# Experts sorted by load on the chip, with capacities of 448, 416, 416 and five times 384 tokens in place of 512 for each

## The chip, the cores and the metric

One core of one Trainium2 chip runs the kernel. The metric is the device time of one execution in microseconds (us); less is better. The profile gives the span from the first to the last instruction of one profiled execution; the device time of that execution lies a little above its span.

## The reference

A recurrent attention block is followed by a mixture of experts. `r`, `k` and `v` have 4 batches, 8 heads, 768 steps and a head size of 48; the attention's output, with heads joined, is a matrix `x` of N = 3072 tokens by 384. Each token goes to the one of 8 experts whose embedding has the largest cosine with it. The expert is a two-layer network (384 to 1024, relu, 1024 to 384), and its output is scaled by the token's softmax weight.

```python
for t in range(S):
    cur = einsum('bhd,bhe->bhde', u * k_t, v_t)
    y[:, :, t] = einsum('bhd,bhde->bhe', r_t, state + cur)
    state = w * state + einsum('bhd,bhe->bhde', k_t, v_t)
x = y.transpose(0, 2, 1, 3).reshape(3072, 384)
logits = normalized(x) @ normalized(expert_emb).T / tau
expert_idx = argmax(logits, axis=1)
gate_w = softmax(logits)[arange(N), expert_idx]
for e in range(8):
    mask = expert_idx == e
    h = maximum(x[mask] @ w1[e], 0)
    out[mask] = gate_w[mask, None] * (h @ w2[e])
```

All is float32. Counted on the reference's own inputs, the experts 0 to 7 get 352, 386, 373, 408, 427, 374, 380 and 372 tokens. After the first 4 of the 6 steps of 128 positions the counts are 247, 251, 253, 271, 272, 248, 256 and 250.

## The kernel before

The attention works in 24 units of 128 tokens (6 chunks of the sequence by 4 batches). The order of the work is written out by hand: `attention` (L544) is a loop over a step `i`, and each step runs one stage of several units. TensorE (PE) transposes r and k (`turn`, L259 and L264), makes scores (`scores`, L277), sums (`sums`, L324 and L327) and states (L294), ScalarE (ACT) copies and makes the diagonal rows (`own_rows`, L249), VectorE (DVE) masks (L281) and adds (`rows`, L340), GpSimd (POOL) scales k (L226) and makes `KU` (L234, L235). Four units of one chunk form a group. For each group `choose`, `ranks`, `gates` and `places` find the expert, the place in the expert's list and the gate of each of its 512 tokens; `cum` holds the running counts (L482). `listed` and `taken` turn places into lists: two one-hot tiles are multiplied on PE (L523, the lanes stationary, 64 columns), and `summed` adds the result to `sums`, a tile of 128 lanes by 2 by 32 slots (token number and gate). An expert has TM = 4 slots of 128 lanes, so 512 places.

PSUM tiles of the attention have one buffer for each tag (two for `tp` and `at`). The tag `st` is shared by the states, by `rank` and by `take`.

The finished rows are stored to DRAM (`put`, L488, on SyncE's DMA queue, SP). The same queue loads K, R and V five units ahead and, in steps 4 and 8, the weights of experts 0 and 1. Constants are made once at the start (`build_consts`), on DVE and POOL, before DVE's first step of unit 0 (L261).

The experts follow in their own order 0 to 7 (L805). For each, POOL gathers four tiles of 128 rows by indirect DMA (L608), PE transposes them (L624, 12 transposes), and DVE copies (L625). The first layer has the weights stationary and 512 tokens as columns: 24 products (L630), each of them two PE instructions in the profile. The second layer has the tokens stationary and 384 output columns: 32 products (L635), again two instructions each. DVE scales by the gate (L637), and POOL scatters 128 rows (L638). The weights have two buffers; those of expert e + 2 are loaded when expert e has released its own (L200, L201). Places with no token are skipped by the bounds check of the DMA.

At the end `needs` counts (L649 to L656) whether an expert has more than 512 tokens, and `again` reads a flag on every engine and jumps past a slow general path, which loops over all experts, unless the flag is set.

Of the kernel before, what the change touches and what calls it, by code (L numbers as in the profile page):

```python
# [18 lines left out]
N = B * S  # L19
# [6 lines left out]
TM = 4  # L26
TT = N // 128
SKIP = 1 << 20
SLOTS = E * TT
W_MIN, W_MAX = 0.7, 1.4  # L30
# [75 lines left out]
def build_consts(k):  # L106
# [33 lines left out]

    k.pos = pool.tile([128, NCH, B], I32, name="pos")
    k.gate = pool.tile([128, NCH, B], F32, name="gate")
    k.sums = pool.tile([128, 2, E * TM], F32, name="sums")
    nc.vector.memset(k.sums, 0.0)

# [51 lines left out]

def load_weights(k, e, tiles):
    w1, w2 = tiles
    k.nc.sync.dma_start(out=w1, in_=k.w1[e].rearrange("(c p) f -> p c f", p=128))  # L200
    k.nc.sync.dma_start(out=w2, in_=k.w2[e].rearrange("(f p) m -> p f m", p=128))  # L201
# [318 lines left out]
def taken(k, g):  # L520
    g.take = k.ps.tile([128, 2, E * TM], F32, name="take", tag="st")
    for b in range(B):
        k.nc.tensor.matmul(  # L523
            g.take.rearrange("p q s -> p (q s)"), g.lane[:, b, :], g.what[:, b].rearrange("p q s -> p (q s)"),
            start=(b == 0), stop=(b == B - 1),
        )


def summed(k, g):
    k.nc.vector.tensor_add(k.sums, k.sums, g.take)  # L530

# [11 lines left out]
def attention(k):  # L543


    units = B * NCH

    def on(f, i):
        if 0 <= i < units:
            f(k, i)  # L550

    def of_group(f, i):
        if 0 <= i < units:
            f(k, k.groups[i // B], i % B)

    def whole(f, i):
        if 0 <= i < units and i % B == B - 1:
            f(k, k.groups[i // B])

    emb = build_experts(k)  # L560
    for i in range(-1, units + 7):
        if 0 < i + AHEAD < units:
            load(k, i + AHEAD)
        if i in (B, 2 * B):
            load_weights(k, i // B - 1, k.weights[i // B - 1])
        if i < 2:
# [12 lines left out]
        on(carry, i)  # L579
        on(rows, i)  # L580
        of_group(put, i)
        on(scores, i + 1)
        on(own_sum, i + 1)
        of_group(turn_rows, i - 1)
        of_group(logits, i - 2)
        whole(ranks, i - 3)
        whole(gates, i - 3)
        whole(taken, i - 5)
        if i == B:
            decays(k)  # L590

# [11 lines left out]
def gather(k, take, gate):  # L603
# [5 lines left out]
        out=G[:, :], out_offset=None, in_=k.xs[:, :], in_offset=IndirectOffsetOnAxis(ap=take, axis=0),  # L609
        bounds_check=N - 1, oob_is_err=False,  # L610
    )
    return G, take, gate


def expert(k, rows, w1, w2):
# [3 lines left out]
    n = 128 * len(rows)  # L619
    xT = k.xtp.tile([128, NK, TM * 128], F32, name="xTe", tag="xTe")  # L620
    for m in range(NK):
        ps = k.ps.tile([128, TM * 128], F32, name="ps", tag="ps")
        for t, (G, _, _) in enumerate(rows):
            nc.tensor.transpose(ps[:, t * 128 : (t + 1) * 128], G[:, m * 128 : (m + 1) * 128], k.ident)  # L624
# [7 lines left out]
    for t, (_, take, gate) in enumerate(rows):  # L632
        ps = k.ps.tile([128, DM], F32, name="ps", tag="ps")
        for f in range(NF):
            mm(ps, hT[:, f, t * 128 : (t + 1) * 128], w2[:, f, :], start=(f == 0), stop=(f == NF - 1))  # L635
        y = k.gp.tile([128, DM], F32, name="y", tag="y", bufs=4)
        nc.vector.tensor_scalar_mul(y, ps, gate)  # L637
        nc.gpsimd.indirect_dma_start(  # L638
            out=k.out[:, :], out_offset=IndirectOffsetOnAxis(ap=take, axis=0), in_=y[:, :], in_offset=None,
            bounds_check=N - 1, oob_is_err=False,  # L640
        )


def needs(k, first):


    nc, pool = k.nc, k.const
    cp = k.ps.tile([128, E], F32, name="ps", tag="ps")
    nc.tensor.matmul(cp, k.ones, k.cum, start=True, stop=True)  # L649
    count = pool.tile([1, E], F32, name="count", tag="count", bufs=2)  # L650
    nc.vector.tensor_sub(count, cp[0:1, :], k.ebase)
    need = pool.tile([1, E, TG], F32, name="need", tag="need", bufs=2)
    for g in range(TG):
        nc.vector.tensor_scalar(need[:, :, g], count, float(TM * 128 * g), None, ALU.is_gt)
    if not first:
        nc.vector.memset(need[:, :, 0], 0.0)  # L656
    return need
# [24 lines left out]
def again(k, need):  # L682


    nc, tc = k.nc, k.tc
# [7 lines left out]
    with tc.If(left > 0):  # L693
        nc.sync.dma_start(out=k.need_dram.rearrange("e g -> (e g)").unsqueeze(0), in_=as_int(k, need))
        far = nc.values_load(flag[0:1, 1:2], min_val=0, max_val=1)
        with tc.If(far > 0):
# [6 lines left out]
            with ExitStack() as ctx:  # L703
                expert_pools(k, ctx)
                nc.sync.dma_start(out=k.need_dram.rearrange("e g -> (e g)").unsqueeze(0), in_=as_int(k, needs(k, True)))
        all_lists(k)
        with ExitStack() as ctx:
            expert_pools(k, ctx)
            with tc.For_i(0, E, 1) as e:
# [7 lines left out]
                nc.sync.dma_start(out=w1, in_=k.w1[bass.ds(e, 1)].rearrange("o (c p) f -> p (o c) f", p=128))  # L717
                nc.sync.dma_start(out=w2, in_=k.w2[bass.ds(e, 1)].rearrange("o (f p) m -> p (o f) m", p=128))
# [36 lines left out]
def kernel(  # L755
# [46 lines left out]
    with ExitStack() as ctx2:  # L802
        expert_pools(n, ctx2)
        take = tiles(n, n.sums, E * TM)
        for e in range(E):  # L805
            at = [gather(n, take[:, j : j + 1], n.sums[:, 1, j : j + 1]) for j in range(e * TM, (e + 1) * TM)]
            expert(n, at, *n.weights.pop(0))
            if e + 2 < E:
                n.weights.append(weight_tiles(n))
                load_weights(n, e + 2, n.weights[-1])  # L810
        need = needs(n, False)
    again(n, need)


# [26 lines left out]
```

## Time and profile before

| | us |
|---|---|
| median of 3 runs | 557.59 |
| lowest, highest | 557.38, 567.32 |
| the profiled execution, device time | 562.05 |
| its span | 560.3 |
| attention, first product to the last list (about) | 0 to 193 |
| first product of the first expert | 202.01 |
| end of the last expert's last product (about) | 545.9 |

The span is the number the parts below add up to. The device time of that execution is 1.75 us above it, and the median of the three runs is 4.46 us below that device time. A row of the chain or of the timeline has a start, a length, an engine and a line of the kernel; a count behind x says how many instructions were merged.

### The profile page before, as it was taken

The numbers are of one execution on the slowest core, as the hardware profiler recorded it, in microseconds if no ns is written. First come the engines' busy times: TensorE is split into PE (matmuls) and PEld (weight loads), VectorE is DVE, ScalarE is ACT, GpSimd is POOL, SyncE is SP. The second block draws the span as 40 slices with busy tenths as digits, with TensorE's granted clock in tenths as the row PEclk, the third lists the DMA queues.
The fourth block names the chain that finished last, engine by engine and source line by source line (L and its number), as shares of the span: only waits on it lengthen the run. The fifth ranks groups of instructions, "written<-read, shape, count | busy, mean of one in ns | idle before, by whom it ended". The sixth has DMA issues, their size and how long they took to land.

```text
span 560.3 us, 7017 instructions
## 1 busy us (share of the span) xinstructions
PE 532.2 (95%) x2625; PEld 355.6 (63%) x2625; DVE 163.1 (29%) x409; ACT 122.1 (22%) x361; POOL 175.5 (31%) x246
## 2 busy tenths in 40 slices
PE   8899999999999589999999999999999999999990
PEld 4899999999999444554554554554554564564550
DVE  6666666666565320030030030030020020010011
ACT  1465444444454002002002002002002102102100
POOL 5856656666651270121122022022022020010010
PEclk9999999999896559999999999999999999999995
DMA  9879796545100040341332322323313312000010
GB/s 188 158 155 305 149 300 133 115 106 115 47 32 30 3 119 1 126 138 44 128 119 69 128 98 82 128 73 112 128 55 131 128 33 106 6 36 1 1 41 8
DMA packets 94590, 54.26 MB, mean 97 GB/s; under 512 B 77741, under 2 KB 89198, under 8 KB 94546
## 3 DMA queue, kind: packets, MB, share of 16 engines
q1 hardware_dynamic: 89024, 43.85, 28.7%
q0 software_dynamic: 4096, 9.45, 5.2%
q10 hardware_dynamic: 1426, 0.41, 0.3%
q8 instruction: 23, 0.38, 0.3%
q14 instruction: 21, 0.17, 0.1%
HBM read 45.83 MB, written 11.01 MB: 101 GB/s over the span
## 4 chain that ended last, share of the span: by engine, by line
PE 91%; DVE 3%; issue 1%; ACT 1%; DMA 1%; POOL 0%; POOLq 0%; ACTq 0%
PE ps L630 30%; PE ps L635 29%; PE y L327 7%; PE at L277 5%; PE y L324 3%; PE st L294 3%; PE lg L433 2%; PE wake L60 2%; PE ps L624 2%; PE xp L418 2%; PE rt L259 2%; PE kt L264 1%; DVE AT L281 1%; PE take L523 1%; ACT xd L249 1%
## 5 line engine op out<-in xcount | busy, mean ns | idle before, releaser
L630 PE MATMUL ps<-xTe,w 128*128 128x512 f32 x384 | 169.6, 602 | 0.5 <-DVE xTe L625 0.5
L635 PE MATMUL ps<-w,hT 128*128 128x384 f32 x512 | 166.4, 486 | 0.0
L635 PEld LDWEIGHTS ps<-w,hT 128*128 128x128 f32 x512 | 97.3, 190 | 69.5 <-issue 3.8
L630 PEld LDWEIGHTS ps<-xTe,w 128*128 128x128 f32 x384 | 73.2, 192 | 92.3 <-issue 86.0
L638 POOL DMA_INDIRECT out_dram<-y,take x32 | 31.7, 991 | 272.9 <-DVE y L637 268.8
L637 DVE TENSOR_SCALAR y<-ps,sums 128x384 f32<-128x384 f32 x32 | 19.8, 618 | 302.5 <-PE ps L635 302.5
L631 ACT ACTIVATE hT<-ps 128x512 f32<-128x512 f32 x64 | 38.2, 597 | 300.7 <-PE ps L630 289.2
L249 ACT ACTIVATE xd<-V,diag 128x48 f32<-128x48 f32 x192 | 45.9, 321 | 20.0 <-DVE diag L241 15.4
L327 PE MATMUL y<-V,AT 128*128 128x48 f32 x384 | 47.5, 278 | 0.0
L327 PEld LDWEIGHTS y<-V,AT 128*128 128x128 f32 x384 | 46.5, 198 | 0.0
L608 POOL DMA_INDIRECT G<-xs,take x32 | 32.6, 1018 | 19.6 <-PE ps L630 8.6
L281 DVE TENSOR_TENSOR AT<-at,umask 128x512 f32<-128x512 f32 x48 | 30.9, 686 | 13.4 <-PE at L277 13.4
L311 POOL TENSOR_TENSOR state<-state,wpow 48x192 f32<-48x192 f32 x40 | 20.4, 509 | 31.1 <-DVE state L307 29.6
L277 PE MATMUL at<-RT,KT 48*128 48x128 f32 x384 | 27.9, 285 | 1.9 <-ACT KT L266 1.9
L277 PEld LDWEIGHTS at<-RT,KT 48*128 48x128 f32 x384 | 23.3, 187 | 3.6 <-ACT KT L266 2.6
L235 POOL TENSOR_TENSOR KU<-KU,Rpad 128x384 f32<-128x384 f32 x24 | 24.1, 1002 | 1.9
L234 POOL TENSOR_TENSOR KU<-K,u_bc 128x384 f32<-128x384 f32 x24 | 23.9, 998 | 0.3 <-DVE diag L241 0.3
L420 ACT COPY xT<-xp 128x384 f32<-128x384 f32 x24 | 11.5, 478 | 56.6 <-PE xp L418 56.6
L226 POOL TENSOR_TENSOR Kpad<-K,kpow 128x384 f32<-128x384 f32 x23 | 22.9, 997 | 1.2
L294 PE MATMUL st<-V,Kpad 128*128 128x96 f32 x160 | 21.7, 281 | 0.7 <-DVE at L478 0.7
L324 PE MATMUL y<-state,RT 128*128 128x96 f32 x160 | 22.0, 282 | 0.0
L294 PEld LDWEIGHTS st<-V,Kpad 128*128 128x128 f32 x160 | 20.3, 199 | 1.4 <-DVE at L478 1.4
(119 smaller groups left out, 393.0 us busy)
## 6 DMA issues: line engine op xcount, KB each, us to landing
w<-in_moe_w_dram SPq DMA_DIRECT2D x16, 1536.0 KB, 7.7
K<-in_k_dram SPq DMA_DIRECT2D x24, 192.0 KB, 3.9
V<-in_v_dram SPq DMA_DIRECT2D x24, 192.0 KB, 4.1
xs<-X SPq DMA_DIRECT2D x24, 192.0 KB, 2.0
Rpad<-in_r_dram SPq DMA_DIRECT2D x23, 192.0 KB, 4.2
G<-xs,take POOLq DMA_INDIRECT x32
out_dram<-y,take POOLq DMA_INDIRECT x32
Rpad<-in_r_dram ACTq DMA_DIRECT2D x1, 192.0 KB, 3.5
```

Of the source, the lines that this page charges most:

```text
L235: nc.gpsimd.tensor_mul(KU, KU, R[:, :, 0:D])
L249: k.nc.scalar.mul(xd[:, h, :], V[:, h, :], diag[:, h : h + 1])
L277: nc.tensor.matmul(at[s][:, p, :], KT[rows, p, :], RT[rows, p, :], start=True, stop=True)
L281: nc.vector.tensor_mul(a, at[s], k.umask[:, None, :].to_broadcast([128, NP, C]))
L294: nc.tensor.matmul(st[:, p, :], pair(Kw, p), pair(V, p), start=True, stop=True)
L324: mm(pair(y, p), RT[:, p, :], T[:, p, :], start=first, stop=False, skip_group_check=True)
L327: mm(y[:, h, :], AT[h % 2][:, h // 2, :], V[:, h, :], start=first, stop=(h == H - 1), skip_group_check=True,)
L608: nc.gpsimd.indirect_dma_start(out=G[:, :], out_offset=None, in_=k.xs[:, :], in_offset=IndirectOffsetOnAxis(ap=take, axis=0), bounds_check ...
L630: mm(ps[:, 0:n], w1[:, m, f * 128 : (f + 1) * 128], xT[:, m, 0:n], start=(m == 0), stop=(m == NK - 1))
L631: nc.scalar.activation(hT[:, f, 0:n], ps[:, 0:n], ACT.Relu)
L635: mm(ps, hT[:, f, t * 128 : (t + 1) * 128], w2[:, f, :], start=(f == 0), stop=(f == NF - 1))
L638: nc.gpsimd.indirect_dma_start(out=k.out[:, :], out_offset=IndirectOffsetOnAxis(ap=take, axis=0), in_=y[:, :], in_offset=None, bounds_chec ...
```

## The change

The lists are kept turned: `taken` has the one-hot of the slots stationary and the lanes as 128 columns, and `sums` is 64 by 128. After four of the six chunks (step 19) one small product counts the tokens of each expert (`counted`), and in step 20 `settle` ranks the counts on DVE. The two experts with the fewest tokens by then are fixed as ranks 7 and 6, their numbers go into a register of SyncE, and their weights are loaded then, in place of the loads in steps 4 and 8. At the end of the attention the counts are taken again, the other six are ranked by load, and a product with a permutation (`turned_lists`, `lists`) turns the lists back, in the order of ranks. The experts run in the ranks' order 7, 6, 5, 4, 3, 2, 1, 0, with capacities of 384 (five times), 416, 416 and 448. The weights of the later ones are read through the register as well. With 384 tokens the expert works as before, with three tiles for four. With 416 or 448 the fourth tile is partial, and the second layer has its weights stationary and the tokens as columns (24 products); ACT copies the result, and PE transposes it back before DVE scales it. Whether an expert passes its capacity is found before the experts begin (`caps_passed`), not after them.

```diff
+CAPS = (448, 416, 416, 384, 384, 384, 384, 384)
+LAST = (7, 6)
+SETTLED = 3
...
+    part = pool.tile([QS, 1], I32, name="part")
+    nc.gpsimd.iota(part, pattern=[[0, 1]], base=0, channel_multiplier=1)
+    bits = pool.tile([QS, 3], I32, name="bits")
...
+    own = pool.tile([QS, 3], F32, name="own")
+    nc.vector.tensor_copy(own, bits)
+    nc.vector.tensor_add(own[:, 1:2], own[:, 1:2], own[:, 2:3])
...
+    nc.vector.scalar_tensor_tensor(k.turned, qt, own[:, 1:2], k.turned, ALU.is_equal, ALU.mult)
+    nc.vector.tensor_scalar_add(k.turned, k.turned, -1.0)
+    k.tie = pool.tile([128, E], F32, name="tie")
+    nc.vector.tensor_scalar(k.tie, k.number, N + 1.0 / 16, None, ALU.mult)
...
+def load_weights_of(k, s, tiles):
+    e = k.nc.sync.value_load(k.who[0:1, s : s + 1], min_val=0, max_val=E - 1)
+    load_weights(k, e, tiles)
...
+def counted(k):
+    cp = k.ps.tile([128, E], F32, name="cp", tag="st")
+    k.nc.tensor.matmul(cp, k.ones, k.cum, start=True, stop=True)
+    return cp
...
-        if i in (B, 2 * B):
-            load_weights(k, i // B - 1, k.weights[i // B - 1])
...
+        if i == SETTLED * B + 7:
+            k.cp = counted(k)
+        if i == SETTLED * B + 8:
+            settle(k, k.cp)
+            for j, s in enumerate(LAST):
+                load_weights_of(k, s, k.weights[j])
+    cp = counted(k)
+    loads, by, perm = turned_lists(k, cp)
+    turned = k.ps.tile([128, 2, E * TM], F32, name="lists", tag="lg")
+    k.nc.tensor.matmul(turned.rearrange("p q s -> p (q s)"), k.sums, perm, start=True, stop=True)
+    k.take = tiles(k, turned, E * TM)
...
+    caps_passed(k, loads, by)
...
-    n = 128 * len(rows)
+    n = sum(r[3] for r in rows)
...
+    if n % 128:
+        yT = k.hp.tile([128, NK, TM * 128], F32, name="yT", tag="yT", bufs=1)
+        for m in range(NK):
+            ps = k.ps.tile([128, TM * 128], F32, name="ps", tag="ps")
+            for f in range(NF):
+                mm(ps[:, 0:n], w2[:, f, m * 128 : (m + 1) * 128], hT[:, f, 0:n], start=(f == 0), stop=(f == NF - 1))
+            nc.scalar.copy(yT[:, m, 0:n], ps[:, 0:n])
+    for t, (_, take, gate, here) in enumerate(rows):
...
+        if n % 128:
+            for m in range(NK):
+                nc.tensor.transpose(ps[0:here, m * 128 : (m + 1) * 128], yT[:, m, at], k.ident)
+        else:
+            for f in range(NF):
+                mm(ps, hT[:, f, at], w2[:, f, :], start=(f == 0), stop=(f == NF - 1))
...
+        turn = list(LAST) + [r for r in reversed(range(E)) if r not in LAST]
+        for i, r in enumerate(turn):
```

DVE at the end of the constants, up to its first step of unit 0 (`RT`). Before:

```order
L94 COPY kpow<-kpT 128x384
L133 MEMSET half 128x4
L102 CAST token<-token_i 128x24
L102 CAST ebase<-ebase_i 1x8
L102 CAST rev<-rev_i 128x8
L102 CAST slots<-slots_i 128x32
L102 CAST lanes<-lanes_i 128x128
L144 MEMSET sums 128x64
L151 MEMSET cum 128x8
L152 COPY cum<-ebase 1x8
L261 TENSOR_TENSOR RT<-rt,rpow 128x512
```

The same place in the changed kernel, from the fourth new step on:

```order
L159 CAST own<-bits 64x3
L160 TENSOR_TENSOR own<-own 64x1
L106 CAST number<-number_i 128x8
L163 TENSOR_SCALAR mask<-number,own 64x8
L106 CAST qt<-qt_i 64x64
L106 CAST turned<-turned_i 64x64
L166 SCALAR_TENSOR_TENSOR turned<-qt,own,turned 64x64
L167 TENSOR_SCALAR turned<-turned 64x64
L170 TENSOR_SCALAR tie<-number 128x8
L180 MEMSET cum 128x8
L181 COPY cum<-ebase 1x8
L296 TENSOR_TENSOR RT<-rt,rpow 128x512
```

Twelve steps stand newly between the `sums` and `cum` fills; `RT` is queued behind them.

DVE in step 20 of the attention, from the last mask to the next row sum. Before:

```order
L281 TENSOR_TENSOR AT_2182<-at,umask 128x512
L241 TENSOR_REDUCE diag<-KU 128x8
L530 TENSOR_TENSOR sums<-sums,take 128x64
L261 TENSOR_TENSOR RT<-rt,rpow 128x512
L340 TENSOR_TENSOR X<-y,xd 128x384
```

In the changed kernel, where `cp` is the PSUM tile of the counts, in the buffer that `take` needs next:

```order
L316 TENSOR_TENSOR AT_2216<-at,umask 128x512
L276 TENSOR_REDUCE diag<-KU 128x8
L577 TENSOR_TENSOR load<-cp,tie 128x8
L584 TENSOR_TENSOR more<-load 128x64
L588 TENSOR_REDUCE by<-more 128x8
L597 TENSOR_SCALAR settled<-by 128x8
L606 TENSOR_TENSOR eq<-by,number 1x64
L610 TENSOR_TENSOR is_e<-eq,number 1x64
L613 TENSOR_REDUCE who<-is_e 1x8
L564 TENSOR_TENSOR sums<-sums,take 64x128
L296 TENSOR_TENSOR RT<-rt,rpow 128x512
L375 TENSOR_TENSOR X<-y,xd 128x384
```

Seven steps of `settle` stand between `diag` and `sums`; PE's `take` of this step comes after `cp` has been read.

DVE between the last list and the first expert. Before:

```order
L530 TENSOR_TENSOR sums<-sums,take 128x64
L597 TENSOR_SCALAR none<-sums 128x32
L599 SCALAR_TENSOR_TENSOR take<-sums,none 128x32
L607 MEMSET G 128x384 x3
L625 COPY xTe<-ps 128x512 x3
```

In the changed kernel:

```order
L564 TENSOR_TENSOR sums<-sums,take 64x128
L577 TENSOR_TENSOR load<-cp,tie 128x8
L581 SCALAR_TENSOR_TENSOR key<-settled,load 128x8
L584 TENSOR_TENSOR more<-key 128x64
L588 TENSOR_REDUCE by<-more 128x8
L623 SCALAR_TENSOR_TENSOR hit,myrank<-by,mask 64x8
L625 TENSOR_SCALAR perm<-turned,myrank 64x64
L727 TENSOR_SCALAR none<-lists 128x32
L729 SCALAR_TENSOR_TENSOR take<-lists,none 128x32
L719 COPY gates<-lists 128x32
```

Six steps, and PE's product `lists` behind them, stand newly ahead of `take`, the index of the gathers; the sixteen steps of `caps_passed` and of the flag follow behind `gates`.

## Rows read from the trace of the kernel before

**Rows 1.** The page: busy us (share of the span) and instructions of each engine.

```profile
PE 532.2 (95%) x2625; PEld 355.6 (63%) x2625; DVE 163.1 (29%) x409; ACT 122.1 (22%) x361; POOL 175.5 (31%) x246
```

**Rows 2.** The chain that ended last: start, us, engine, tile, line.

```profile
202.01 23.51 PE ps L630 x48
225.52 20.64 PE ps L635 x64
246.16 1.31 PE ps L624 x12
247.47 20.87 PE ps L630 x48
...
525.24 20.66 PE ps L635 x64
```

**Rows 3.** Busy time by stretches: us, PE, PEld, DVE, ACT, POOL, granted clock, DMA share, GB/s.

```profile
146.00:147.00 1.00, 1.00 (x7) 1.00 (x6) 0.64 (x5) 0.82 (x5) 0.65 (x4) 0.50 0.00 0
176.00:190.00 14.00, 11.24 (x54) 11.04 (x53) 7.64 (x37) 4.24 (x16) 2.84 (x7) 0.50 0.04 14
228.00:231.00 3.00, 3.00 (x11) 1.81 (x10) 0.28 (x1) 0.00 (x0) 0.00 (x0) 1.00 1.04 427
```

**Rows 4.** The page: instruction groups (busy, mean ns) and DMA issues (KB, us to landing).

```profile
L635 PEld LDWEIGHTS ps<-w,hT 128*128 128x128 f32 x512 | 97.3, 190 | 69.5 <-issue 3.8
L631 ACT ACTIVATE hT<-ps 128x512 f32<-128x512 f32 x64 | 38.2, 597 | 300.7 <-PE ps L630 289.2
w<-in_moe_w_dram SPq DMA_DIRECT2D x16, 1536.0 KB, 7.7
```

**Rows 5.** Timeline of the start: start, us, engine, line, operation.

```profile
11.25 2.28 DVE L152 COPY cum<-ebase 1x8 f32<-1x8 f32 x1
11.57 0.98 POOL L226 TENSOR_TENSOR Kpad<-K,kpow 128x384 f32<-128x384 f32 x1
12.52 0.99 POOL L234 TENSOR_TENSOR KU<-K,u_bc 128x384 f32<-128x384 f32 x1
13.53 0.69 DVE L261 TENSOR_TENSOR RT<-rt,rpow 128x512 f32<-128x512 f32 x1
13.59 0.99 POOL L235 TENSOR_TENSOR KU<-KU,Rpad 128x384 f32<-128x384 f32 x1
14.61 1.16 PE L277 MATMUL at<-RT,KT 48*128 48x128 f32 x16 [0.68 <-ACT KT L266]
16.57 1.00 POOL L235 TENSOR_TENSOR KU<-KU,Rpad 128x384 f32<-128x384 f32 x1
```

**Rows 6.** Timeline of step 20 and of PE's next scores.

```profile
159.76 1.08 PE L523 MATMUL take<-what,lane 128*128 128x64 f32 x8
160.10 0.54 DVE L241 TENSOR_REDUCE diag<-KU 128x8 f32<-128x384 f32 x1
161.33 0.69 DVE L261 TENSOR_TENSOR RT<-rt,rpow 128x512 f32<-128x512 f32 x1 [0.23 <-PE rt L259]
164.27 1.16 PE L277 MATMUL at<-RT,KT 48*128 48x128 f32 x16
```

**Rows 7.** Timeline between the last list and the first expert.

```profile
186.20 0.60 PE L456 MATMUL rank<-oh,umask 128*128 128x32 f32 x2 [1.27 <-DVE l L448]
193.32 0.18 DVE L597 TENSOR_SCALAR none<-sums 128x32 f32<-128x32 f32 x1
193.54 0.19 DVE L599 SCALAR_TENSOR_TENSOR take<-sums,none 128x32 int32<-128x32 f32 x1
195.59 1.01 POOL L608 DMA_INDIRECT G<-xs,take  x1 [0.31 <-issue]
```

**Rows 8.** Timeline of the end.

```profile
545.92 0.62 DVE L637 TENSOR_SCALAR y<-ps,sums 128x384 f32<-128x384 f32 x1 [4.54 <-PE ps L635]
546.63 0.60 DVE L654 TENSOR_SCALAR need<-count 1x8 f32<-1x8 f32 x6
546.81 0.98 POOL L638 DMA_INDIRECT out_dram<-y,take  x1 [4.18 <-DVE need L654]
```

More of the change, by code (lines that the diff above doesn't have):

```diff
@@ new lines, in settle, with expert_of @@
+def settle(k, cp):
+    nc, pool = k.nc, k.const
+    _, by = order(k, cp)
+    k.settled = pool.tile([128, E], F32, name="settled")
+    nc.vector.tensor_scalar(k.settled, by, float(min(LAST)) - 1, None, ALU.max)
+    expert_of(k, by)
+def expert_of(k, by):
+    nc, pool = k.nc, k.const
+    full = [1, E, E]
+    eq = pool.tile(full, F32, name="eq", tag="eq", bufs=2)
+    nc.vector.tensor_tensor(
+        eq, by[0:1, None, :].to_broadcast(full), k.number[0:1, :, None].to_broadcast(full), ALU.is_equal
+    )
+    is_e = pool.tile(full, F32, name="is_e", tag="is_e", bufs=2)
+    nc.vector.tensor_mul(is_e, eq, k.number[0:1, None, :].to_broadcast(full))
+    k.who = pool.tile([1, E], I32, name="who", tag="who", bufs=2)
+    with nc.allow_low_precision(reason="whole numbers, one of each sum's terms not zero"):
+        nc.vector.reduce_sum(k.who, is_e, axis=AX.X)
+    return eq
@@ new lines, in turned_lists, with caps_passed @@
+def turned_lists(k, cp):
+    nc, p = k.nc, k.rt
+    load, by = order(k, cp, k.settled)
+    hit = p.tile([QS, E], F32, name="hit", tag="hit")
+    rank = p.tile([QS, 1], F32, name="myrank", tag="myrank")
+    nc.vector.scalar_tensor_tensor(hit, by[0:QS], 1.0, k.mask, ALU.mult, ALU.mult, accum_out=rank)
+    perm = p.tile([QS, QS], F32, name="perm", tag="perm")
+    nc.vector.tensor_scalar(perm, k.turned, rank, None, ALU.is_equal)
+    return load, by, perm
+def caps_passed(k, load, by):
+    nc, pool = k.nc, k.const
+    eq = expert_of(k, by)
+    full = [1, E, E]
+    cap_of = pool.tile(full, F32, name="cap_of")
+    nc.vector.tensor_mul(cap_of, eq, k.caps[:, :, None].to_broadcast(full))
+    over = pool.tile([1, E], F32, name="over")
+    nc.vector.reduce_sum(over, cap_of.rearrange("o s e -> o e s"), axis=AX.X)
+    nc.vector.tensor_tensor(over, load[0:1], over, ALU.is_gt)
+    k.need = grouped(k, load[0:1])
+    nc.vector.tensor_mul(k.need, k.need, over[:, :, None].to_broadcast([1, E, TG]))
@@ L533, in route, with grouped @@
+def grouped(k, load):
+    need = k.const.tile([1, E, TG], F32, name="need", tag="need", bufs=2)
+    for g in range(TG):
+        k.nc.vector.tensor_scalar(need[:, :, g], load, float(TM * 128 * g), None, ALU.is_gt)
+    return need
 def route(k, g):
@@ L600, in tiles, with gather @@
     return take
-def gather(k, take, gate):
+def gather(k, take, gate, n=128):
     nc = k.nc
@@ L622, in expert @@
         ps = k.ps.tile([128, TM * 128], F32, name="ps", tag="ps")
[L623 to L624 removed]
+        for t, (G, _, _, here) in enumerate(rows):
+            nc.tensor.transpose(
+                ps[:, t * 128 : t * 128 + here], G[0:here, m * 128 : (m + 1) * 128], k.ident[0:here, 0:here]
+            )
         nc.vector.tensor_copy(xT[:, m, 0:n], ps[:, 0:n])
@@ L803 @@
         expert_pools(n, ctx2)
-        take = tiles(n, n.sums, E * TM)
-        for e in range(E):
-            at = [gather(n, take[:, j : j + 1], n.sums[:, 1, j : j + 1]) for j in range(e * TM, (e + 1) * TM)]
+        turn = list(LAST) + [r for r in reversed(range(E)) if r not in LAST]
+        for i, r in enumerate(turn):
+            at = [
+                gather(n, n.take[:, j : j + 1], n.gates[:, j : j + 1], min(128, CAPS[r] - t))
+                for t, j in zip(range(0, CAPS[r], 128), range(r * TM, (r + 1) * TM))
+            ]
             expert(n, at, *n.weights.pop(0))
-            if e + 2 < E:
+            if i + 2 < E:
                 n.weights.append(weight_tiles(n))
-                load_weights(n, e + 2, n.weights[-1])
-        need = needs(n, False)
-    again(n, need)
+                load_weights_of(n, turn[i + 2], n.weights[-1])
+    again(n)
 _INS = ['r', 'k', 'v', 'w', 'u', 'moe_expert_emb', 'moe_tau', 'moe_w1', 'moe_w2']
```

80 lines of the change are left out of this document (48 added, 32 removed).

## The prediction

> **What bounds the kernel now.** I read the page first: PE is busy for 95% of the span and no other engine comes near it [rows 1]. The chain that ended last says where. From 202.01 us on it is PE alone: for each expert 12 transposes, 48 instructions of the first layer, 64 of the second, with nothing between them [rows 2]. The reader should see there that the expert part (202.01 to 545.90, 343.9 us) is as long as the columns that PE streams, and nothing else. A second-layer instruction with 384 columns takes 20.64 / 64 = 322.5 ns, a first-layer one with 512 columns 20.87 / 48 = 434.8 ns, so 0.877 ns for each further column [rows 2]. The weight load beside it takes 190 ns [rows 4], less than either, so fewer columns do mean less time down to far below 384. The first expert's first layer took 23.51 us instead of 20.87: the granted clock, which was 0.50 (the lower level, 1.2 GHz) through the routing's tail, came back only some microseconds into the dense work [rows 2, 3]. The weights are no bound: 1536 KB land 7.7 us after their issue, with the DMA engines full meanwhile [rows 3, 4], and two such loads have a whole expert's time.
>
> **The experts.** By the counts of the reference's inputs, every expert fits its rank's capacity. Experts 0 and 5 are the smallest after four chunks and end at 352 and 374; the others, sorted, have 427, 408, 386, 380, 373 and 372 tokens. So no slow path is run.
> - Capacity 384, five times: 48 + 48 instructions of 322.5 ns are 30.96 us, and 9 transposes at 1.31 / 12 us [rows 2] are 0.98: 31.94 each, 159.7 together. Before it was 42.82.
> - Capacity 416, twice: 350.6 ns an instruction (322.5 + 32 x 0.877), 96 of them are 33.66 us. Transposes in cost 1.31 at most (a partial one can't cost more than a full one) and the 12 transposes back another 1.31. Before the last of these PE waits for ACT's copy, 0.60 us for 512 columns [rows 4]; I take 0.6 for the wait, since two transposes lie beside it. 36.9 each, 73.8.
> - Capacity 448, last: 96 x 378.6 ns + 1.31 = 37.7 up to its last product.
>
> With the first expert's slow clock (2.64, kept) and without its transposes, which lie before 202.01, that is 159.7 + 73.8 + 37.7 + 2.6 - 1.0 = 272.8 against 343.9: **-71.1 us**.
>
> **The end.** Before, the last product is followed by DVE's scaling and one scatter on POOL, issued by 547.79, 1.9 us later; the six steps of the needs end at 547.23 and the flag a little after [rows 8]. Now the last expert's four tiles all come after its last product: ACT's copy 0.6, a transpose 0.3 with its latency, DVE 0.62, 0.27 to POOL, then four scatters, of which three cost 1.31 (1.01 and a pause of 0.31, the rate of POOL's gathers [rows 7]) and the last 0.98: 6.7 us. **+4.8 us**. The flag is ready early, but what follows POOL's last issue (12.5 us to the span's end) is as long as before, since the scatter is what it now waits for.
>
> **The start.** The twelve new steps on DVE are small, but `RT` is queued behind them. In the trace a copy of 1 x 8 values, `cum`, is issued at 11.25 and ends at 13.53, 2.28 us, and 13.53 is the pause between POOL's two dependent products for `KU` (12.52 to 13.51, then 13.59) [rows 5]. I read this as DVE waiting for POOL, which works without a pause from 11.57 on. It cost nothing, because `RT` can start only then anyway. Now several such steps stand in a row: the two `TENSOR_SCALAR` on `turned` and `tie`, and the copy of `cum`, float32 from SBUF to SBUF like the step that waited. If each of the three needs a pause of POOL, they get those at 13.53, just ahead of 16.57 (between the next dependent pair) and at 17.57, after POOL's last product of this stretch, and `RT` starts near 17.6 [rows 5]. PE's first scores wait for `RT` and ACT alone, so what is late there is late in the end: the first steps are a chain through PE, DVE and ACT with no slack. **+4 us**. Bounds: 0, if DVE gets all three through the first pause or doesn't wait at all; 9, if PE's idle time also lowers the granted clock and the next 10 us run at half.
> The Trainium skill (SBUF — State Buffer, "Who interferes with whom") says that a float32 copy or `tensor_scalar` within SBUF takes a port pair that GpSimd also needs, and that the one that comes second is blocked for the other's whole instruction. It says the same of DVE steps with two SBUF inputs against GpSimd's reads, which would add two of the new steps (`own`, `turned`) to the three; by it `RT` starts near 18 and this term would be +4.5.
>
> **Step 20.** The counts `cp` sit in the one PSUM buffer that `take` needs, and DVE reads them only after `diag`, which ends at 160.64 [rows 6]. PE would start `take` at 159.76 and so waits until about 160.9: 1.1 us, behind it `rt`, `kt` and the next sums. The other six steps of `settle`, at 0.22 each (the distance of two dependent steps, 193.32 and 193.54 [rows 7]), end about 162.2, when PE's `rt` is done too, so `RT` loses little more. If they wait for POOL as above, `RT` is 3 us later, of which nearly 2 are hidden, since the scores at 164.27 need it only 2.2 us after it was done. I take **+1.5**, bounds 0 (DVE reads early enough) and +6 (POOL in the way, and a drop of the clock, which did fall to 0.50 in this part of the attention once before, at 146 [rows 3]). Behind SP's wait for `who` stand three stores of finished rows and nothing else. The weights, four loads, are issued by 168 at the latest and take less than 20 us, the stores behind them are down by some 190, and the first gather can't start before `take` is done, 193.73 [rows 7]. So the weights cost nothing there, and their old places cost nothing before.
>
> **The boundary.** Six dependent steps of 0.22 on DVE and a product as that of `rank` (0.60 at the lower clock [rows 7]) with 0.2 for the hand-overs stand ahead of the gathers: +2.1. The product of the counts lies beside `sums`. The first expert waits for three gathers, not four: -1.31 [rows 7]. **+0.9**, bounds 0 and +3. The sixteen steps of `caps_passed` run while the gathers land.
> The same page of the Trainium skill warns that such DVE steps keep GpSimd from writing the descriptors of its own DMAs. The trace doesn't show it: six `need` steps on DVE took 0.60 us beside a scatter, which took its usual 0.98 [rows 8]. By the rule the gathers could lose the steps' whole time, 16 x 0.2 = 3.2 us.
>
> **Sum.** -71.1 + 4.8 + 4 + 1.5 + 0.9 = -59.9. From the profiled execution's 562.05 that gives 502.2. The median of the runs stands 4.46 below that execution; with the same distance the prediction is **497.7 us**.
>
> **The rivals.**
> - The start hides it all. For: no row says that a pause of POOL lets only one step of DVE through. Against: the 2.28 us. Price: without the +4, 493.7.
> - The two new pauses of PE lower the clock for longer. For: in the routing's tail it stayed at 0.50 all through 176 to 190 although PE was busy for 11.2 of 14 us [rows 3], so this mix of small products doesn't always bring it back. Against: after 146 it recovered within a few us. A stretch of 14 us at half costs up to 7: 505.
> - DVE's checks hold up the gathers, as the page has it: +3.2, 500.9.
> - The experts gain only half, for a cause not seen here (a wait for weights or gathers in each): 533. Against: the DMA engines had room, and 190 ns is below 322.
> - Slower than before: an expert passes its capacity by one token, and the general path runs. It decides at 384 for rank 3, which has 380 tokens, a margin of 4; rounding in the cosine could move one or two. Price: eight rounds of weights that nothing hides, 8 x 2 x 7.7 = 123 us, and one expert again, 42.8, over 660 in all.
>
> **How the numbers follow.** My forecast, with its own small errors (495 to 500), has 0.46, the hidden start 0.25, the clock 0.18, the held gathers 0.06, the half gain 0.03, the general path 0.01, and 0.01 that nothing changes. The range of 490 to 508 leaves out the last three, half of the clock's upper end, and a little below. A measurement of this kernel tells about 2% from no change; only the general path is slower by that, only the last case lies within it, and every other case is faster: 0.98, 0.01, 0.01.
>
> **What would show it.** Right: first- and second-layer instructions 322 ns apart for five experts, about 351 and 379 for the three with partial tiles; 32 us for each of five experts; four scatters in a row at the end, and some 19 us from the last product to the span's end. At the start, a DVE step of 1 to 3 us among the new constants, and the first scores near 18.6. In step 20, PE's `take` waiting for `load`. Wrong: a product that waits for weights or gathers between experts, an expert's columns that take longer than 0.85 ns each, a granted clock of 0.5 for long stretches before 170, or the flag set.

## The result, and the profile after

| | before | after |
|---|---|---|
| median of the runs, us | 558.87 (557.38 to 567.32) | 510.08 (509.36 to 511.29) |
| profiled execution, us | 562.05 | 509.36 |
| its span, us | 560.3 | 507.5 |

The ratio is 0.914, with a 95% interval of 0.910 to 0.918: the kernel is faster by some 9%. One of the four runs before, that of 567.32 us, was slow and is left out of the ratio. The prediction said 497.7 with a range of 490 to 508, and 510.08 lies above it. The direction was right, the size was not: the span fell by 52.8 us, where the sum had said 59.9.

Where the 52.8 went is read best by cutting the span at two points, the first product of the first expert and the last product of the last one.

| stretch | before | after | difference | predicted |
|---|---|---|---|---|
| start of the span to the first expert's first product | 202.01 | 210.01 | +8.0 | +6.4 |
| experts, first to last product | 343.9 | 275.0 | -68.9 | -71.1 |
| last product to the end of the span | 14.4 | 22.5 | +8.1 | +4.8 |

The first view is the timeline of PE in the experts of the changed kernel: one expert of capacity 384, then the last one, of 448.

```profile
242.18 1.15 PE L754 MATMUL ps<-ident,G 128*128 128x128 f32 x9
243.52 15.75 PE L762 MATMUL ps<-xTe,w 128*128 128x384 f32 x48 [0.20 <-DVE xTe L757]
259.11 15.64 PE L780 MATMUL ps<-w,hT 128*128 128x384 f32 x48
274.59 1.15 PE L754 MATMUL ps<-ident,G 128*128 128x128 f32 x9
...
448.69 18.31 PE L762 MATMUL ps<-xTe,w 128*128 128x448 f32 x48 [0.37 <-DVE xTe L757]
466.83 18.20 PE L770 MATMUL ps<-hT,w 128*128 128x448 f32 x48
484.87 1.66 PE L777 MATMUL ps<-ident,yT 128*128 128x128 f32 x12
```

From one row of transposes to the next are 32.41 us, against 42.82 before [rows 2]. Nothing waits there but 0.2 us for DVE's copy of the transposed rows. The last product ends at 485.03. Before, 64 second-layer instructions with 384 columns stood at this place; now there are 48 with 448, and all rows of the result come after them.

The second is the timeline of the start, DVE with the POOL and PE rows beside it; it answers to [rows 5].

```profile
12.19 2.08 DVE L159 CAST own<-bits 64x3 f32<-64x3 int32 x1
13.26 0.98 POOL L269 TENSOR_TENSOR KU<-K,u_bc 128x384 f32<-128x384 f32 x1
14.31 0.15 DVE L160 TENSOR_TENSOR own<-own 64x1 f32<-64x1 f32 x1
14.33 1.01 POOL L270 TENSOR_TENSOR KU<-KU,Rpad 128x384 f32<-128x384 f32 x1
14.38 0.97 DVE L106 CAST number<-number_i 128x8 f32<-128x8 int32 x1
15.29 0.99 POOL L261 TENSOR_TENSOR Kpad<-K,kpow 128x384 f32<-128x384 f32 x1
15.39 0.92 DVE L163 TENSOR_SCALAR mask<-number,own 64x8 f32<-64x8 f32 x1
16.33 0.98 DVE L106 CAST turned<-turned_i 64x64 f32<-64x64 int32 x1
17.34 1.07 DVE L166 SCALAR_TENSOR_TENSOR turned<-qt,own,turned 64x64 f32<-64x64 f32 x1
18.75 0.16 DVE L181 COPY cum<-ebase 1x8 f32<-1x8 f32 x1
18.82 0.67 DVE L296 TENSOR_TENSOR RT<-rt,rpow 128x512 f32<-128x512 f32 x1
19.64 2.08 PE L312 MATMUL at<-RT,KT 48*128 48x128 f32 x16 [4.96 <-DVE RT L296]
26.66 1.16 PE L312 MATMUL at<-RT,KT 48*128 48x128 f32 x16
```

Five steps, which take 0.16 to 0.27 us where POOL is idle (e9 below), show 0.9 to 2.1 us each, and each of these ends as a POOL instruction ends: the first three at 14.27, 15.35 and 16.31, where 14.24, 15.34 and 16.28 are ends of the three POOL rows. `cum` at 18.75, behind POOL's last product of this stretch, takes 0.16 us again. `RT` starts at 18.82 instead of 13.53, the first scores at 19.64 instead of 14.61, and these take 2.08 us instead of 1.16. The windows of the changed kernel (columns as in [rows 3]) show why:

```profile
14.00:20.00 6.00, 1.04 (x10) 0.83 (x10) 5.32 (x12) 0.58 (x1) 4.17 (x5) 0.81 1.33 195
20.00:24.00 4.00, 4.00 (x28) 3.78 (x26) 2.15 (x7) 0.49 (x3) 0.00 (x0) 0.50 0.30 41
24.00:28.00 4.00, 4.00 (x41) 3.83 (x40) 2.33 (x6) 1.89 (x8) 2.40 (x4) 0.93 0.02 6
```

PE was busy for 1.04 of 6 us while it waited for `RT`, and the granted clock then stood at 0.50, the lower level, until about 24.

The third is the end: POOL's scatters of the last expert, and one line of the view of waits (total us, count, longest).

```profile
486.92 0.99 POOL L783 DMA_INDIRECT out_dram<-y,take  x1 [29.10 <-DVE y L782]
490.64 0.98 POOL L783 DMA_INDIRECT out_dram<-y,take  x1 [2.74 <-DVEq L822]
493.98 0.98 POOL L783 DMA_INDIRECT out_dram<-y,take  x1 [2.37 <-DMA out_dram<-y,take]
497.32 0.94 POOL L783 DMA_INDIRECT out_dram<-y,take  x1 [2.36 <-DMA out_dram<-y,take]
```

```profile
POOL out_dram L783 <- DMA out_dram<-y,take: 17.7, 6, 5.8
```

The scatters stand 3.34 to 3.72 us apart, not 1.31: POOL waits until the transfer of the one before has landed. For the first of the three pauses the profile names the jump past the general path (DVEq L822) instead; at the same place in e7 and e9 it is the landing as well (3.25 and 3.34 us). The kernel's own text has no wait there, and no run here issues the scatters without it, so whether it comes from the order that the program keeps for writes to one tensor, or from the queue, is not shown. Before, a scatter came every 5.16 us behind its own products, so this wait never showed; the 4.18 us of idle time in [rows 8] ended with DVE's work.

Last, step 20 and the boundary in PE's timeline, which answer to [rows 6, 7].

```profile
167.24 1.06 PE L558 MATMUL take<-lane,what 128*64 128x128 f32 x8 [0.95 <-DVE load L577]
...
197.17 1.97 PE L558 MATMUL take<-lane,what 128*64 128x128 f32 x8 [2.55 <-POOL what L547]
199.51 0.60 PE L569 MATMUL cp<-cum,ones 128*128 128x8 f32 x2 [0.37 <-DVE sums L564]
201.56 0.69 PE L716 MATMUL lists<-perm,sums 64*128 64x64 f32 x2 [1.45 <-DVE perm L625]
```

Before, the last `take` stood at 191.06:

```profile
191.06 1.97 PE L523 MATMUL take<-what,lane 128*128 128x64 f32 x8 [2.55 <-POOL what L512]
```

And three windows of the changed kernel to set beside those of before at 146 and from 176 to 190 [rows 3], where the clock stood at 0.50:

```profile
146.00:150.00 4.00, 4.00 (x40) 3.95 (x37) 2.62 (x10) 2.90 (x11) 1.49 (x4) 1.00 0.72 138
...
172.00:180.00 8.00, 8.00 (x86) 7.71 (x86) 5.68 (x15) 3.85 (x13) 0.00 (x0) 1.00 1.02 359
180.00:190.00 10.00, 8.66 (x60) 8.22 (x59) 5.61 (x24) 3.89 (x15) 2.52 (x7) 0.75 1.05 389
```

The lower level comes later here, so the last steps of the attention run faster than before. The DMA share of 1.02 and 1.05 is the weights, loaded here now; PE is busy beside them.

### The profile page after: what moved, and what is told of

It reads as the page before. It is cut to its first block, busy times and chain, and to the rows that moved or that the text cites. A ratio compares the mean times of both kernels' runs of the same rounds, so it can differ in the third digit from the quotient of the medians.

```text
span 507.5 us, 6873 instructions
## 1 busy us (share of the span) xinstructions
PE 463.7 (91%) x2522; PEld 331.6 (65%) x2522; DVE 164.4 (32%) x431; ACT 120.7 (24%) x370; POOL 166.3 (33%) x248
## 5 line engine op out<-in xcount | busy, mean ns | idle before, releaser
L762 PE MATMUL ps<-xTe,w 128*128 128x384 f32 (+2 forms) x384 | 132.2, 505 | 1.8 <-DVE xTe L757 1.8
L762 PEld LDWEIGHTS ps<-xTe,w 128*128 128x128 f32 x384 | 73.0, 192 | 57.5 <-issue 22.5
L783 POOL DMA_INDIRECT out_dram<-y,take x27 | 26.6, 986 | 227.7 <-DVE y L782 202.5
L782 DVE TENSOR_SCALAR y<-ps,gates 128x384 f32<-128x384 f32 (+2 forms) x27 | 15.8, 614 | 243.7 <-PE ps L780 141.2
L763 ACT ACTIVATE hT<-ps 128x384 f32<-128x384 f32 (+2 forms) x64 | 32.2, 503 | 208.7 <-PE ps L762 208.7
L780 PE MATMUL ps<-w,hT 128*128 128x384 f32 x240 | 78.2, 486 | 0.0
L780 PEld LDWEIGHTS ps<-w,hT 128*128 128x128 f32 x240 | 45.6, 190 | 31.8
L770 PE MATMUL ps<-hT,w 128*128 128x416 f32 (+1 forms) x144 | 52.1, 521 | 0.0
L362 PE MATMUL y<-V,AT 128*128 128x48 f32 x384 | 45.8, 273 | 0.0
L770 PEld LDWEIGHTS ps<-hT,w 128*128 128x128 f32 x144 | 27.4, 190 | 24.2 <-issue 24.2
L738 POOL DMA_INDIRECT G<-xs,take x27 | 27.5, 1018 | 19.3 <-issue 6.1
```

The costliest lines, as they stand in the source:

```text
L362: mm(y[:, h, :], AT[h % 2][:, h // 2, :], V[:, h, :], start=first, stop=(h == H - 1), skip_group_check=True,)
L738: nc.gpsimd.indirect_dma_start(out=G[0:n, :], out_offset=None, in_=k.xs[:, :], in_offset=IndirectOffsetOnAxis(ap=take[0:n], axis=0), bound ...
L762: mm(ps[:, 0:n], w1[:, m, f * 128 : (f + 1) * 128], xT[:, m, 0:n], start=(m == 0), stop=(m == NK - 1))
L763: nc.scalar.activation(hT[:, f, 0:n], ps[:, 0:n], ACT.Relu)
L770: mm(ps[:, 0:n], w2[:, f, m * 128 : (m + 1) * 128], hT[:, f, 0:n], start=(f == 0), stop=(f == NF - 1))
L780: mm(ps, hT[:, f, at], w2[:, f, :], start=(f == 0), stop=(f == NF - 1))
```

## The experiments

Eleven runs follow, e1 to e11. An experiment's ratio is against the kernel before on the same chip. My theory: the missing 7 us are in the start (DVE behind POOL, then the lower clock), in the scatters, and a little in each expert, and the 4.46 us between profiled execution and median were no property of the kernel. The rivals are named with each run.

**e1: the kernel before once more.** No edit.

> The kernel before, profiled once more, to see how far one profiled execution stands from another. If the 4.46 us between the first profile and the median were a fixed price of profiling, this one lies near 560.3 us of span again. If they were one execution's own luck with the granted clock, the span lies 2 to 5 us lower, and the difference is found in a stretch with another granted clock (the drop at 146, or the time at which the clock returns in the first expert).

Measured: 561.95 us, span 560.2. Beside it, seven runs of the same kernel on that chip went from 558.97 to 566.6. The span is the one that a fixed price of profiling would give, but the other runs on that chip lie on both sides of it (their median is 562.35), and the profiled executions of e4 to e10 lie between 0.4 below and 1.1 above the medians of their own runs. So the 4.46 us are no price of profiling. What they are, e3 shows below.

**e2, e3: six more DVE steps at the start of the kernel before**, copies in one, sums in the other (the loop is shortened here; each kernel has one of the two lines):

```diff
     no_counts(k)
+    for x in range(6):
+        nc.vector.tensor_copy(d[:, x], k.rev)                            # e2
+        nc.vector.reduce_sum(d[:, x, 0:1], k.rev, axis=AX.X)             # e3
```

> The kernel before, with six float32 copies of 128 x 8 values in SBUF put on DVE behind the copy of the counts, ahead of its first step of unit 0. Theory (such a step waits for a pause of POOL): each of them ends with an instruction of POOL, the first scores start at 17 to 19.5 us in place of 14.6, and the span grows by 3 to 7. Rival (they cost their own time): 0.1 us each, first scores at 14.6 to 15.4, nothing to be seen in the span.

> As the run with six copies, but six sums over 128 x 8 values each, from the same tile. Theory (only steps that need what POOL uses are held up): 0.1 to 0.2 us each, first scores at 14.6 to 15.4. Rival (any step of DVE at this place is held up, whatever it reads): as with the copies, 17 us or later.

Measured, one run each: e2 563.87 us, span 562.1, first scores at 15.67; e3 558.63 us, span 556.8, first scores at 14.37. DVE's timeline, the kernel with copies and then the one with sums:

```profile
12.79 2.14 DVE L155 COPY more<-rev 128x8 f32<-128x8 f32 x6
14.85 0.67 DVE L269 TENSOR_TENSOR RT<-rt,rpow 128x512 f32<-128x512 f32 x1
```

```profile
13.14 0.48 DVE L155 TENSOR_REDUCE more<-rev 128x1 f32<-128x8 f32 x6
13.55 0.67 DVE L269 TENSOR_TENSOR RT<-rt,rpow 128x512 f32<-128x512 f32 x1
```

Six copies took 2.14 us, six sums of the same shape 0.48. So the wait belongs to the kind of step, not to DVE's queue or to the number of its instructions. The six copies got by with two waits for POOL, so the first scores came earlier than the 17 to 19.5 that I expected. The new constants of the change waited five times; that they needed more because they depend on each other is my reading, not shown.

e3 shows more. The windows where the clock of before fell (mean 0.58 from 146 to 150, 0.65 from 172 to 176) look like this there:

```profile
146.00:150.00 4.00, 3.77 (x35) 3.53 (x32) 2.10 (x8) 2.93 (x12) 3.69 (x8) 1.00 0.01 4
172.00:176.00 4.00, 3.50 (x33) 3.40 (x31) 2.66 (x14) 2.12 (x10) 0.77 (x4) 1.00 0.01 4
```

The clock stays at 1.00, the first expert begins at 198.84, 3.2 us earlier than in [rows 2], and the span is 3.5 us shorter, though six sums were added and the first scores are only 0.24 us earlier. So a difference of this size lies in the granted clock of the attention, which falls in some executions of this kernel and not in others. That the 4.46 us are of this kind is likely and not shown, since none of the three runs left a trace. The other runs of the kernel before fit: those with a mean granted clock of 0.964 and more took 557.3 to 560.7 us, those with 0.948 to 0.956 took 562.0 to 566.6. It also means that the span differences of e2 and e3 are not the price of their steps; the start of the timeline is.

**e4: all of the change but its smaller capacities.** With 512 for every rank, the sorting, the settling and the turned lists stay, and PE's work in the experts is as before.

```diff
-CAPS = (448, 416, 416, 384, 384, 384, 384, 384)
+CAPS = (512,) * 8
```

> The changed kernel with all eight capacities at 512, so that the sorting, the late weights and the turned lists are there and nothing is saved. Theory (the change's overhead before the experts is 8 us, of which 6.6 at the start, and its long end comes from the partial last expert alone): first product of the first expert near 210, experts 42.8 us each as before, the end as before or up to 3 us shorter, span 565 to 569. Rival (sorting the experts costs in the experts too, or the long end comes from the early flag): experts above 43 us, or 20 us and more from the last product to the end.

Measured: 568.94 us against 562.35, ratio 1.012 (1.006 to 1.018), span 566.7. The chain that ended last shows its first expert at 211.01, 9.0 us later than in [rows 2], then the same 343.6 us, then 12.1 to the end instead of 14.4.

```profile
211.01 23.22 PE ps L762 x48
...
533.95 20.66 PE ps L780 x64
```

The machinery alone costs 6 to 7 us: 9.0 ahead of the experts, 2.3 of which come back behind the last product. So the columns are the whole gain.

**e5, e9: the new constants where DVE has nothing to do.** In e5 POOL's new counters come first of all its constants and DVE's steps follow `rpow`:

```diff
     nc.vector.tensor_mul(k.rpow, t, over_i)
+    early_consts(k)
```

> The changed kernel with its new constants made earlier, while DVE waits for PE and POOL has nothing to do (behind the powers of the decay). Theory (the start lost 6 us because DVE's steps waited for POOL and PE's clock fell meanwhile): first scores at 14.5 to 16 in place of 19.6, no stretch at half clock behind them, span 501 to 503. Rival (the lateness is made up later, or comes from the steps' number): span 506 or more.

Measured: 502.43 us, span 500.4, `RT` at 13.23, first scores at 14.31. What this kernel leaves in the output is not the reference's, for a reason that I didn't find, so its time is read for the start alone. e9 keeps POOL's old order of instructions and emits all of them ahead of the powers, DVE's steps again behind `rpow`.

> The changed kernel with GpSimd's part of the constants in its old order but emitted ahead of the decay powers, and VectorE's new steps put behind the powers, where VectorE waits for the transposed powers anyway (7.9 to 10.4 us in the changed kernel). Theory (the start cost is VectorE's wait at GpSimd's pauses plus the half clock that follows from the later first scores): the new steps take 1 to 1.5 us between 7.8 and 9.4 without a wait, the first RT starts at 13.2 to 14.3 instead of 18.82, the first scores at 14.3 to 15.3 instead of 19.64, span 500 to 502. Rival (what is late at the start is only hidden slack, or the first expert's clock takes it back): span 504 to 508.

Measured: 504.38 us, ratio 0.902 (0.893 to 0.911), span 502.5. The timelines of DVE and PE in e9:

```profile
6.89 0.16 DVE L113 CAST number<-number_i 128x8 f32<-128x8 int32 x1
...
7.17 0.22 DVE L158 TENSOR_SCALAR mask<-number,own 64x8 f32<-64x8 f32 x1
...
7.38 0.27 DVE L161 SCALAR_TENSOR_TENSOR turned<-qt,own,turned 64x64 f32<-64x64 f32 x1
...
13.64 0.69 DVE L326 TENSOR_TENSOR RT<-rt,rpow 128x512 f32<-128x512 f32 x1
14.72 1.16 PE L342 MATMUL at<-RT,KT 48*128 48x128 f32 x16 [0.68 <-ACT KT L331]
...
203.56 8.69 PE L792 MATMUL ps<-xTe,w 128*128 128x384 f32 x20 [0.22 <-issue]
```

The same steps that took up to 2.08 us now take 0.16 to 0.27, with POOL idle beside them, and the granted clock stays at 1.00 from 14 to 24. The first expert begins 6.45 us earlier than in the changed kernel; 0.64 of it is the copy of `kpow`, which starts earlier (10.24 against 10.88) and which moves from run to run, so the start's cost is 5.8. That is good to about 1 us: e8 has the changed kernel's start 0.94 earlier, and its first expert begins 0.25 later, after a stretch with the clock at 0.83 (160 to 170). The span fell by 5.0 only, to just above the expected 500 to 502: the first expert took 0.9 longer, as the rival's second half had it, and the pause behind the first of the last scatters was 0.6 us longer.

**e6, e8: the end.** In e6 an expert of capacity 384 comes last, the partial ones in the middle. In e8 the turn stays, but the last expert's second layer is in the old form, rows as tokens, 64 instructions of 384 columns.

```diff
-        turn = list(LAST) + [r for r in reversed(range(E)) if r not in LAST]
+        turn = list(LAST) + [0, 1, 2, 5, 4, 3]                           # e6
...
-    if n % 128:
+    turned = n % 128 and not last                                        # e8
+    if turned:
...
```

> The changed kernel with the ranks in the order 7, 6, 0, 1, 2, 5, 4, 3, so that an expert of 384 tokens comes last and its scatters are 5 us apart. Theory (each scatter waits until the one before has landed, 3.3 us, and only a last expert with all its tiles at the end shows that): from the last product to the end 11 to 12 us in place of 22.5, the partial experts as long as before, span 496 to 498. Rival (POOL's rate of 1.3 us a scatter is what counts): only 4 us less, span 503.

> The changed kernel with the last expert's second layer in the form of before: tokens stationary, 384 columns, also for its partial tile of 64 tokens. Its products cost 20.6 us in place of 18.2 and the transposes of 1.5, but the scatters come 5 us apart. Theory (scatters wait for landings): the end from the last product 11 to 12 us, span 498 to 499.5. Rival (only POOL's rate of 1.3 us counts): 504 or more.

Measured: e6 501.48 us, ratio 0.897 (0.893 to 0.900), span 500.5; e8 502.03, 0.899 (0.895 to 0.902), span 499.9. POOL's last scatters of e6:

```profile
479.96 0.99 POOL L783 DMA_INDIRECT out_dram<-y,take  x1 [21.10 <-DVE y L782]
485.12 0.98 POOL L783 DMA_INDIRECT out_dram<-y,take  x1 [4.17 <-DVE y L782]
490.28 0.98 POOL L783 DMA_INDIRECT out_dram<-y,take  x1 [4.18 <-DVE y L782]
```

They are 5.16 us apart again, each behind its own products, and only one follows the last product (489.35). From there to the end of the span are 11.1 us in e6 and 11.2 in e8, against 22.5: the partial form at the last place cost 11.3. Both spans are above what was expected (496 to 498, 498 to 499.5), and below both rivals. In e6, 4.2 us of the gain went elsewhere: its experts took 279.2 us, since the first one was 1.6 longer, and the product of a full expert now has to wait for a partial one's rows once more (3.66 us from the last product of one to the first of the next instead of 1.18). e8 paid 2.7 for 64 instructions instead of 48 (20.95 against 18.20), and 0.6 in its first expert.

**e7: the settling at the end of step 19.**

```diff
-            k.cp = counted(k)
-        if i == SETTLED * B + 8:
-            settle(k, k.cp)
+            settle(k, counted(k))
```

> The changed kernel with settle moved from step 20 to the end of step 19, so that the counts are read before the next lists need their PSUM buffer. Theory (PE's wait of 0.95 us for the counts is all that settle costs): 0.9 to 1.3 us less, span 506.3. Rival (DVE's steps of settle then delay its step for the next scores): 0 to 1 us more.

Measured: 507.78 us, span 507.1. PE's `take` of step 20 no longer waits, and from the scores ahead of it to those behind it 6.80 us pass (163.63 to 170.43) instead of 7.79 (164.08 to 171.87): 1.0 us, the step's cost. The first expert begins at 208.99, 1.0 us earlier, of which 0.3 is an earlier copy of `kpow` (10.57); 0.5 is lost again between the first two scatters. So the span fell by 0.4 us, less than the expected 0.9 to 1.3.

**e10: the three together**, constants as in e9, the small expert last as in e6, the settling as in e7.

> The constants behind the powers, the counting settled one step earlier, and an expert of 384 as the last in the turn, all three together. Theory (the three costs lie one behind the other on the path that sets the end, so they add): 507.5 less 6.5 for the start, less 1.0 for the wait in step 20, less 7.0 for the end: span 492 to 494.5, 494 to 496.5 us by the clock. Rival (the costs overlap, or the clock at the first expert takes some back): span 496 to 500.

Measured: 493.76 us, ratio 0.882 (0.874 to 0.889), span 491.9, just below what was expected. The costs lie one behind the other and add up, stretch by stretch: 8.1 us ahead of the experts, where e9 and e7 gave 6.45 and 1.0, and 11.1 behind the last product, where e6 gave 11.3, less 3.6 in the experts, where e6 lost 4.2.

```profile
201.93 17.86 PE ps L790 x48
...
465.05 15.49 PE ps L808 x48
```

This chain begins 8.1 us ahead of the changed kernel's and ends with 11.4 us behind the last product. It is the fastest version in this study.

**e11: each of the last four scatters made twice**, with the same rows and values.

```diff
+        for _ in range(2 if last else 1):
             nc.gpsimd.indirect_dma_start(
```

> The changed kernel with each of the four scatters of the last expert made twice, the same rows and values again. Theory (a scatter is issued only when the one before has landed, 3.3 to 3.7 us apart): four more of 3.3 us, span 507.5 + 13.4 = 520 to 522. Rival, the step as the prediction had it (POOL issues them one after the other, 1.31 us each): 507.5 + 5.2 = 512 to 513.5. Second rival (the bytes set it): the second of a pair lands beside the first, span 508 to 511.

Measured in one run: 521.26 us, span 519.5. POOL's timeline:

```profile
486.96 0.99 POOL L784 DMA_INDIRECT out_dram<-y,take  x1 [29.11 <-DVE y L782]
...
496.74 0.98 POOL L784 DMA_INDIRECT out_dram<-y,take  x1 [1.87 <-DMA out_dram<-y,take]
500.09 0.98 POOL L784 DMA_INDIRECT out_dram<-y,take  x1 [2.37 <-DMA out_dram<-y,take]
502.94 0.98 POOL L784 DMA_INDIRECT out_dram<-y,take  x1 [1.86 <-DMA out_dram<-y,take]
...
508.89 0.91 POOL L784 DMA_INDIRECT out_dram<-y,take  x1 [1.67 <-DMA out_dram<-y,take]
```

Four more scatters lengthened the span by 12.0 us, 3.0 each, where the issue rate of the prediction would give 5.2 in all. It is 0.5 less than the theory's lowest, since a repeat follows in 2.6 to 2.9 us in three of its four places. Each waits for the DMA of the one before: the rival in which they overlap falls.

## Why the prediction was wrong, and where it was right

The distance is 510.08 - 497.7 = 12.4 us. Of it 7.1 are the sum, 52.8 against 59.9, and 5.2 the step from the profiled execution to the median; 0.1 is lost in rounding and between span and device time.

- **The experts (2.2 of the 7.1).** Right in their mechanism: time goes with columns, and no product waits for weights or gathers between experts. The instructions with 416 and 448 columns took what was worked out (18.2 us for 48 of the latter). Mis-sized were the transposes with the wait for `xTe` behind them: 1.34 instead of 0.98 in an expert of 384 (242.18 to 243.52), 2.43 instead of 1.31 ahead of the last one. So a later expert of 384 took 32.4 (31.94), the partial ones 37.0 and 37.5 (36.9), the last 38.8 up to its last product (37.7). The first expert gave 1.4 back: 32.17 against 33.6, since its clock rose sooner than before.
- **The end (3.3).** The step that failed is "three cost 1.31 (1.01 and a pause of 0.31, the rate of POOL's gathers)". I took the rate of transfers that only read for transfers that write the same tensor, and those wait for each other's landing, 3.3 to 3.7 us. From the last product to the last scatter's issue it took 13.2 us instead of 6.7, +6.5. "What follows POOL's last issue is as long as before" failed too, in the other direction: 9.2 us instead of 12.5. e11 shows the price of a scatter, e4 the shorter tail, e6 and e8 that the form and the turn decide whether the wait shows.
- **Ahead of the experts (1.6).** Three terms and a gain that the sum didn't have. *The start*: the mechanism and its place were right, and the bounds of 0 and 9 held it; +4 was mis-sized, e9 shows 5.8, so the rival of a hidden start falls. I counted three steps of the kind that waited in the row I had, so that `RT` would start near 17.6. Those three (`TENSOR_SCALAR` on `turned` and `tie`, the copy of `cum`) took 0.15 to 0.19 us each, behind POOL's last product. What waited were the casts `own`, `number` and `turned`, the step on `mask` and the `SCALAR_TENSOR_TENSOR` on `turned`; that three wrong steps gave nearly the right time is luck. `RT` is 7.94 us behind the copy of `kpow` instead of 3.40 (18.82 - 10.88, 13.53 - 10.13), 4.5 more. The half clock behind it, which I had kept for the upper bound, came and cost 1.4. (The copy of `kpow` itself started anywhere from 9.48 to 10.93 in the traces of this study, also with an unchanged start; the 0.75 by which it is later here I don't put down to the change.) The Trainium skill's rule (SBUF — State Buffer, "Who interferes with whom") names casts beside copies and `tensor_scalar` as steps that can contend with GpSimd, and says that `tensor_reduce` on this chip never does. The casts (up to 2.08 us) and e3's sums (0.48 us for six) agree. I had left the casts out when I counted by it, so that my +4.5 met the measured 4.5 is luck too: of the five steps counted, one waited. *Step 20*: right, 1.0 to 1.2 against 1.5, with the wait of `take` at the place named. Two of its steps did wait for POOL (`more` 1.05 us, `settled` 0.73), but `RT` was done at 170.60, before the scores at 171.87. *The boundary*: from the last `take` to the first product 12.84 us instead of 10.95, +1.9 against +0.9 (whose own working, 2.1 - 1.31, gives 0.8). What failed there is "The product of the counts lies beside `sums`": it came behind `sums`, with PE waiting for that step, and the counts were read (200.14) 0.7 us after `sums` was done (199.46). These terms make more than the +8.0 of the table. The rest came back: before had dropped to the lower clock at 146 and from about 173 on, after only from about 185, so the scores of step 18 are 7.3 late (149.99 against 142.69), those of step 20 6.4 (164.08 against 157.70), and the last `take` 6.1 although step 20's wait lies between. This gain is not the change's own: against e3, which is the kernel before without these drops, the first expert of the changed kernel begins 11.2 us later (210.01 against 198.84), 1.05 of them for its `kpow`.
- **Held gathers.** The rival falls: the gathers are 1.62 and 1.32 us apart beside the comparisons with the capacities on DVE, against 1.56 and 1.31 for the same pairs before (from 194.03 on), which is at most 0.1 lost.
- **The median.** "With the same distance" failed. The distance of one execution from a median of three was taken as a property that the changed kernel would share. By e3 it is most likely the clock, which had fallen in the attention of the execution profiled before; after's profiled execution lies 0.7 below its median. The forecast should have had 502.2, the sum without the distance, as its middle; 7.9 us would still have been missing.

What stays open is why the clock of the kernel before falls at 146 in some executions, why it rises at different moments in the first expert when the work ahead of it is the same (33.5, 34.1 and 35.2 us from its first product to the next expert's in the changed kernel, e8 and e6), what makes the scatters wait for each other, and what went wrong in e5.

## What to carry to other kernels

Cutting streamed columns gave what the columns were worth, but a new form of the last tile moves all its output behind the last product, so the tile that ends the kernel should be one whose results leave while it still computes. Scatters to one tensor, issued one behind the other as here, cost their landing each and not their issue. Small constants belong where VectorE and GpSimd are both idle: the same steps cost 5.8 us at one place and nothing 5 us earlier. And a forecast that starts from one profiled execution carries that execution's clock: see whether its low stretches are in the other runs too.

## What was unexpected in the hardware

- On DVE, casts from int32 to float32, a `TENSOR_SCALAR` and a step with two inputs waited for POOL's instruction to end (0.92 to 2.08 us for steps of 0.16 to 0.27 us); six sums of 128 x 8 values beside the same POOL work took 0.48 us in all.
- Consecutive scatters to one tensor were 3.3 us apart, with 0.98 us of issue each and the landing of the one before as what ended POOL's idle time; gathers were 1.31 us apart.
- After 4.96 us in which PE waited, its clock was granted at 0.50 for the next 4 us, with PE busy throughout.
- The kernel before has two courses of the clock in its attention: 0.50 from 146 to 149 and again from 173 (before, e1), or 1.00 up to 176 (e3), with 3.2 us between them at the first expert.
